# Groups four to seven of the first layer: from eight block products to seven in the first pass

## The chip, the cores and the metric

One core of one Trainium2 chip runs the whole program. The metric is the device time in microseconds (us) of one execution; the times below are of the same program executed several times.

## The reference

Attention without softmax, normed, and then two feed-forward blocks, all in float32:

```python
kv  = einsum('bhsd,bhse->bhde', k, v); out = einsum('bhsd,bhde->bhse', q, kv)   # 8 x 8 heads, 576 tokens, 64 wide
x   = out / sqrt(mean(out*out) + 1e-6) * g_norm                                 # then 4608 tokens x 512
h   = x @ w_in;  x = softplus(h) @ w_out                                        # 512 -> 2048 -> 512
h   = maximum(maximum(x @ w1, x @ w2), x @ w3);  y = h @ w2_out                 # 3 times 512 -> 768, then -> 512
```

## The kernel before, in words

The 4608 tokens are worked on in five passes of two half passes of 456 or 464 tokens (NS, L19). Every float32 operand is split in two parts, "hi" (a rounded copy) and "lo" (what is left), and a product is three matmuls: hi by hi, hi by lo, lo by hi (`mm3`, L150).

A layer is worked on in **groups** of 256 x 256 weights by the two half passes; a group is a 2 x 2 matrix of 128-row weight blocks a11, a12, a21, a22 times a 2 x 2 matrix of inputs. The first layer has eight groups H0 to H7 (numbers g = 0 to 7), the second eight, X00 to X31 (g = 8 to 15), the three of the second block nine (g = 16 to 24), the last layer three (g = 25 to 27). There are two ways to compute a group:

- **Plain**: eight block products. `plain_group` (L758) and `plain_sum` (L413) make each of the four results in a PSUM bank of its own, X and Y in turn, out of 12 matmuls (2 x 2 x 3). A group is 48 matmuls. Weights are a11, a12 (PLAIN[0]) and a21, a22 (PLAIN[1]), split as they are.
- **Seven products**: `run_group` (L403) and `product` (L390) run seven products of 6 matmuls in the order of ORDER (L37): m1 to bank X, m5 to bank Y, m6 on top of X, m2 to bank W, m7 on top of X, m4 on top of X, m3 on top of Y. A group is 42 matmuls. It takes sums of the weight blocks (`weight_sum`, L312, on GpSimd), sums of the inputs (`combine`, L370), and sums of results (`sums`, L424): after m1, m6 and m7 ScalarE copies bank X to SBUF before the next product goes on top of it, and VectorE adds banks W and Y later. SLOT (L36) places the products at 0, 1, 3, 4, 6, 9 and 12 steps from the group's start, and groups start 7 steps apart, so the last two products of a group stand between the first of the next.

In the first pass all groups are plain, and that pass also prepares the weights for the others: `convert` (L301) turns a raw double-precision block into float32 (two ScalarE and two VectorE instructions), `split_blocks` (L337) splits the plain blocks, `sums_of_weights` (L324) makes the four sums of a group in place, further `split_blocks` split the sums, and `keep_blocks` (L343) stores every split block to DRAM. Passes two to five load these units (`load_unit`, L206) and run all groups with seven products.

The order of the work is written out by hand. Everything is an event with a time in steps (`at`, L177); the events are issued in order of time. Up to t = 1 a string of names (OPENING, L43) sets the order on all engines, groups H0 to H2 of the first pass among them; after it the SP queue (all loads and stores) goes in order of events, and the other engines in the order that the scheduler gives at build time, earlier events first among those that it holds for ready. `order` (L737) places the groups of the first pass; `weights_at` (L708) places the weights' work around a group's start t; `x_plain`, `h_plain` (L774) evict results: ScalarE's softplus in the bank, ScalarE's cast to hi, VectorE's subtraction to lo. `plain_out` (L946) is the last layer of the first pass. Rings of buffers: PSUM banks X 2, Y 2, W 1, at 2, cv 1 (L100); two-block weight tiles "u" 4; weight sums "sw" 3; raw blocks 3; the inputs' tiles "xc" 28, the layer results' "gc" 28, the short-lived "c" 10.

In a row's names X, Y and W are the banks, followed by h for the first layer, x for the second, o for the three of the second block and y for the last.

Of the kernel before, what the change touches and what calls it, by code (L numbers as in the profile page):

```python
# [8 lines left out]
F32 = mybir.dt.float32  # L9
# [28 lines left out]
U_BUFS, U3_BUFS, GE_BUFS = 4, 2, 14  # L38
LATE = 23
OPEN, PIN, GATE = -100, 1, 24  # L40
ENGINES = tuple(getattr(mybir.EngineType, e) for e in ("PE", "Activation", "DVE", "Pool", "SP"))
LEAD = 10
OPENING = """  # L43
# [21 lines left out]
def kernel(  # L65
# [36 lines left out]
    def psum(tag, name):  # L102
        return ps.tile([P, 512], F32, tag=tag, bufs=PS_BUFS[tag], name=name)
# [4 lines left out]
    def ctile(name, n, dtype=F32):  # L108
        return wide(cp, "c", 10, name, n, dtype)
# [4 lines left out]
    def gc_tile(name, n, dtype=F32):  # L114
        return wide(gp, "gc", 28, name, n, dtype)
# [18 lines left out]
    def cast(eng, hi, src):  # L134
        if eng is nc.scalar:
            nc.scalar.copy(hi, src)  # L136
        else:
            eng.tensor_copy(hi, src)

    def split(eng_hi, src, hi, lo, eng_lo):  # L140
        cast(eng_hi, hi, src)
        eng_lo.tensor_tensor(out=lo, in0=src, in1=hi.bitcast(F32), op=ALU.subtract)  # L142
# [4 lines left out]
    def sub(eng, o, a, b):  # L147
        eng.tensor_tensor(out=o, in0=a, in1=b, op=ALU.subtract)  # L148
# [16 lines left out]
    def with_table(name, out, src, func, **kw):  # L165

        if tables["set"] != name:
            with after(tables["used"]):
                load = nc.scalar.preload_act_table_set(name)
            tables.update(set=name, load=load.ins, used=[])  # L170
        with after([tables["load"]]):
            tables["used"].append(nc.scalar.activation(out, src, func, **kw).ins)
# [4 lines left out]
    def at(t, fn, *args):  # L177
        events.append((t, len(events), fn, args))
# [14 lines left out]
    def unit_tile(size, p, own=False):  # L193
        if own and "ge" in pools:
            uxs.append(pools["ux"] if "ux" in pools and len(uxs) % 2 else pools["ge"])
            return uxs[-1].tile([P, 2, 512], F32R, tag="ux", bufs=1, name="ux")
        if size == 2:
            return up.tile([P, 2, 512], F32R, tag="u", bufs=U_BUFS, name="u")
        return up.tile([P, 1, 512], F32R, tag="u3", bufs=U3_BUFS, name="u3")

    def keep(key, u):
        n = u.shape[1] * 512
        wd[key] = dr.tile([P, n], F32, tag=f"wd{len(wd)}", name=f"wd{len(wd)}")
        nc.sync.dma_start(out=wd[key], in_=u.rearrange("p i n -> p (i n)").bitcast(F32))
# [36 lines left out]
    def raw_of(g):  # L241
        if g < 8:
            return [w_in[2 * g + i] for i in range(2)]
        if g < 16:
            return [w_out[2 * (g - 8) + i] for i in range(2)]
        if g in G_O:
            return [w2_out[2 * (g - G_O[0]) + i] for i in range(2)]
        f, j = divmod(g - 16, 3)
        return [w123[2 * f + i, j] for i in range(2)]
# [9 lines left out]
    def rebase(key, halves=(0, 1), tag=None):  # L259

        raw = raws[key]
        lo32, hi32 = raw[:, :, 0], raw[:, :, 1]
        if 0 in halves:
            t = parts[key] = psum(tag or ("W" if key[1] and key[0] < 17 else "cv"), "cv")
            nc.scalar.activation(t, hi32.bitcast(F32), AF.Copy, scale=2.0**-112)
        if 1 in halves:
            nc.scalar.activation(lo32, lo32.bitcast(U32), AF.Copy, scale=LOW_SCALE, bias=LOW_BIAS)
# [18 lines left out]
    sw = {}  # L286
# [50 lines left out]
    def split_blocks(g, ms, eng):  # L337

        u = unit_tile(len(ms), 0)
        split(nc.scalar, blocks_of(g, ms), u[:, :, 0:256], u[:, :, 256:512], eng)  # L340
        plain[g, ms] = u

    def keep_blocks(g, ms, of):  # L343
        u = plain[g, of]
# [58 lines left out]
    def run_group(base, p, g, rhs, after, slot=SLOT):  # L403
        banks = {}

        def step(m):
            product(p, g, m, rhs, banks)
            after(m, {k: v[:, 0:NS[p]] for k, v in banks.items()})

        for m in sorted(ORDER, key=slot.get):  # L410
            at(base + slot[m], step, m)
# [242 lines left out]
    def x_tiles(pas, c):  # L654
        a, n = TOK[pas], NS[pas]
        return [og_t[a + t * n, c + 2 * r] for r in range(2) for t in range(2)]
# [45 lines left out]
    def run_pass(pas, base):  # L702
# [3 lines left out]
        R = xc.setdefault(pas, {})  # L706

        def weights_at(t, g, slot=SLOT):  # L708
            if pas == 0:
                if g not in (0, 1, 2, 8):  # L710
                    for i in range(2):
                        jobs.append((t - 6 + 2.7 * i, (g, i), raw_of(g)[i], convert, (g, i)))
                    at(t - 3.4, split_blocks, g, PLAIN[0], nc.vector)
                    at(t - 0.6, split_blocks, g, PLAIN[1], nc.vector)
                if g > 1:
                    at(t + 0.2, sums_of_weights, g)
                if g >= LATE:
                    at(t + 4, keep_sums, g)
                    return
                if g < 2:  # L720
                    return
                for ms, dt in (((5, 6), 2.6), ((7,), 3.8), ((3,), 4.6)):
                    at(t + dt, split_blocks, g, ms, nc.gpsimd)
                    at(t + dt + 2.9, keep_blocks, g, ms, ms)
                if g not in (2, 8):
                    at(t + 0.5, keep_blocks, g, (1, 2), PLAIN[0])
                    at(t + 3, keep_blocks, g, (4,), PLAIN[1])
            else:
                for k, ms in enumerate(UNITS):

                    own = k == 0 and g != 17
                    lead = (8 if g == 0 else 5.9 if pas == 1 else 9) if own else LEAD
                    at(t + min(slot[m] for m in ms) - lead, load_unit, pas, (g, k), len(ms), own)
# [1 line left out]
        order = ["H0", "H1", "H2", "H3", "X00", "X01", "H4", "H5", "X10", "X11", "H6", "H7",  # L735
                 "X20", "X21", "X30", "X31"]
        if pas == 0:  # L737
            order = ["H0", "H1", "H2", "X00", "X01", "H3", "H4", "X10", "X11", "H5", "H6", "X20", "H7", "X21",
                     "X30", "X31"]
        start = {name: base + 7 * i for i, name in enumerate(order)}  # L740

# [16 lines left out]
        def plain_group(t, g, rhs, done, halves_first=False):  # L758
            outs = [(i, k) for i in range(2) for k in range(2)]
            if halves_first:  # L760
                outs = [(i, k) for k in range(2) for i in range(2)]

            def step(i, k, tag):
                done(i, k, plain_sum(g, i, k, rhs, tag))

            for n, (i, k) in enumerate(outs):
                at(t + 1.75 * n, step, i, k, "XY"[n % 2])

        def split_here(acc, tile):
            hi, lo = tile("hi", N, F32R), tile("lo", N, F32R)  # L770
            split(nc.scalar, acc, hi, lo, nc.vector)
            return hi, lo

        def h_plain(fp, i, k, acc):  # L774
            with_table(PLUS_SET, acc, acc, AF.Softplus)
            gc.setdefault(fp // 2, {})[i, k, fp % 2] = split_here(acc, xc_tile if fp == 7 else gc_tile)

        for fp in range(8):
            t = start[f"H{fp}"]
            weights_at(t, G_H[fp])  # L780
            if pas == 0:
                if fp > 2:
                    plain_group(t, G_H[fp], R0, partial(h_plain, fp))
                continue
            run_group(t, pas, G_H[fp], R, sums(lambda w, src, fp=fp: h_done(fp, w, src), lambda w: (ctile(f"h{w}", N), w != 11),
                           nc.vector if fp == 0 else nc.scalar))
# [158 lines left out]

        def plain_out(t):  # L946
            for j, (g, ts, split_at, sums_at) in enumerate(zip(
                    G_O, ((-8.6, -7), (-5, -3.2), (2, 4.5)), ((-6.2, -4.8), (-1.9, 0.1), (5.3, 7.05)), (1, 3.5, 9))):
                for i in range(2):
                    jobs.append((t + ts[i], (g, i), raw_of(g)[i], convert, (g, i)))  # L950
                    at(t + split_at[i], split_blocks, g, PLAIN[i], nc.vector if (j, i) == (1, 1) else nc.gpsimd)
                at(t + sums_at, sums_of_weights, g)
                at(t + sums_at + 3, keep_out, g)
            for n in range(8):
                e, i, k = n // 4, n // 2 % 2 if n > 3 else n % 2, n % 2 if n > 3 else n // 2 % 2
                at(t + 2.63 * n, out_plain, e, i, k, "XY"[n % 2])
                at(t + 2.63 * n + 5, out_store, e, 11 + 10 * i + k)
# [58 lines left out]

    def x_lo(k, eng):
        h, p = divmod(k, NP)
        low(eng, *tile_of.pop(k), og_t.pop((h * n0, p)))

    def low(eng, hi, lo, src):
        sub(eng, lo, src, hi.bitcast(F32))
# [177 lines left out]
```

## Time and profile before

| what | value |
|---|---|
| device time, median of 3 | 1377.56 us (1376.12 to 1379.06) |
| the profiled execution: its own time | 1378.63 us |
| its span, first to last instruction | 1376.8 us |
| TensorE busy in the span | 1359.8 us (99%), 6646 matmuls |
| VectorE, ScalarE, GpSimd busy | 826.7, 753.4, 649.6 us |
| data moved by DMA | 336.59 MB, mean 244 GB/s |

The span is what the profile sees; 1.8 us of the execution lie outside it. PE is TensorE's matmuls, DVE VectorE, ACT ScalarE, POOL GpSimd, SP the queue that issues the DMAs. A busy TensorE is not proof of TensorE at its best, since its matmuls overlap; the step from one matmul's start to the next is the better measure.

### The profile page before, as it was taken

To read this page: it belongs to the slowest core of one execution; us is meant where nothing else is said; L and a number is where in the kernel's file an instruction comes from. 1 tells how busy PE (TensorE), PEld (TensorE's weight loads), DVE (VectorE), ACT (ScalarE), POOL (GpSimd) and SP (SyncE) were. 2 spreads that over 40 slices of the span, in tenths; PEclk is the share of its full clock that TensorE was granted. 3 is DMA by queue.
4 is the path that set the end of the run, shared out by engine and by line. 5 is a ranking of instruction groups with operands and counts; after the bars stand their busy time and mean duration, and the time that the engine had idled before them with its cause. 6 is when DMAs were issued, how large, how long until landed. Compare 5 with 4: busy or idle time off the path is not lost.

```text
span 1376.8 us, 19727 instructions
## 1 busy us (share of the span) xinstructions
PE 1359.8 (99%) x6646; PEld 1212.5 (88%) x6646; DVE 826.7 (60%) x1307; ACT 753.4 (55%) x1461; POOL 649.6 (47%) x611
## 2 busy tenths in 40 slices
PE   8999999999999999999999999999999999999998
PEld 6799999888888888888888988888888889998897
DVE  6866657884445766745546667445567754457544
ACT  6786637884655457546444575464346645443332
POOL 3876545666555535335346253453334534445320
PEclk9999999999999999999999999999999999999999
DMA  8699868877899777586667764866676577666665
GB/s 302 226 340 310 313 237 296 273 248 253 300 333 329 263 271 247 169 301 211 214 213 251 259 210 161 295 212 214 208 225 198 188 259 236 212 206 204 219 199 171
DMA packets 132084, 336.59 MB, mean 244 GB/s; under 512 B 14224, under 2 KB 34576, under 8 KB 131984
## 3 DMA queue, kind: packets, MB, share of 16 engines
q1 hardware_dynamic: 131408, 334.36, 72.8%
q8 instruction: 53, 0.87, 0.3%
q10 hardware_dynamic: 576, 0.98, 0.2%
q14 instruction: 47, 0.39, 0.1%
HBM read 269.88 MB, written 65.40 MB: 244 GB/s over the span
## 4 chain that ended last, share of the span: by engine, by line
PE 88%; DMA 4%; DVE 3%; ACT 3%; POOL 1%; issue 1%; SPq 0%; DVEq 0%; ACTq 0%; POOLq 0%
PE Xx L152 5%; PE Xx L154 5%; PE Xx L153 5%; PE Xo L152 5%; PE Xh L152 5%; PE Xh L154 5%; PE Xh L153 5%; PE Xo L154 5%; PE Xo L153 5%; PE Yx L154 3%; PE Yx L153 3%; PE Yx L152 3%; PE Yh L152 3%; PE Yh L154 3%; PE Yh L153 3%; PE Yo L152 2%
## 5 line engine op out<-in xcount | busy, mean ns | idle before, releaser
L142 POOL TENSOR_TENSOR lo<-e,hi 128x464 fp32r<-128x464 f32 (+1 forms) x160 | 187.1, 1203 | 178.1 <-ACT hi L136 171.4
L136 ACT CAST hi<-t 128x464 fp32r<-128x464 f32 (+1 forms) x120 | 65.4, 546 | 114.9 <-DVE e L148 44.1
L152 PE MATMUL Xo<-hi,u 128*128 128x464 f32 (+1 forms) x296 | 111.6, 378 | 0.0
L154 PE MATMUL Xo<-hi,u 128*128 128x464 f32 (+1 forms) x296 | 110.0, 372 | 0.4 <-DVE u L142 0.4
L153 PE MATMUL Xo<-lo,u 128*128 128x464 f32 (+1 forms) x296 | 109.8, 371 | 0.0
L152 PE MATMUL Xh<-hi,u 128*128 128x464 f32 (+1 forms) x262 | 97.7, 373 | 2.9 <-DVE lo L148 1.7
L142 DVE TENSOR_TENSOR lo<-t,hi 128x464 fp32r<-128x464 f32 (+1 forms) x120 | 75.9, 637 | 38.3 <-ACT hi L136 36.0
L136 ACT COPY m<-Xo 128x464 f32<-128x464 f32 (+1 forms) x108 | 58.4, 546 | 73.0 <-PE Xo L154 72.8
L145 DVE TENSOR_TENSOR x<-x,Xx 128x464 f32<-128x464 f32 (+1 forms) x104 | 65.6, 632 | 52.9 <-PE Xx L154 52.6
L153 PE MATMUL Xh<-lo,u 128*128 128x464 f32 (+1 forms) x262 | 97.1, 371 | 0.0
L154 PE MATMUL Xh<-hi,u 128*128 128x464 f32 (+1 forms) x262 | 97.1, 370 | 0.0
L136 ACT CAST hi<-e 128x464 fp32r<-128x464 f32 (+1 forms) x160 | 85.4, 581 | 19.7 <-PE Yx L153 16.3
L152 PE MATMUL Xx<-hi,u 128*128 128x464 f32 (+1 forms) x256 | 95.1, 372 | 0.0
L154 PE MATMUL Xx<-hi,u 128*128 128x464 f32 (+1 forms) x256 | 94.9, 371 | 0.0
L153 PE MATMUL Xx<-lo,u 128*128 128x464 f32 (+1 forms) x256 | 94.8, 370 | 0.0
L142 POOL TENSOR_TENSOR u<-sw,u 128x256 fp32r<-128x256 f32 (+1 forms) x68 | 69.1, 1031 | 38.2 <-ACT u L136 38.1
L142 POOL TENSOR_TENSOR lo<-m,hi 128x464 fp32r<-128x464 f32 (+1 forms) x40 | 47.8, 1214 | 79.9 <-ACT hi L136 79.9
L148 POOL TENSOR_TENSOR e<-e 128x464 f32<-128x464 f32 (+1 forms) x32 | 38.0, 1189 | 99.4 <-DVE t L148 99.4
L136 ACT CAST u<-sw 128x512 fp32r<-128x512 f32 (+1 forms) x119 | 62.3, 537 | 37.2 <-POOL sw L148 16.3
L148 POOL TENSOR_TENSOR sw<-sw 128x256 f32<-128x256 f32 x84 | 67.9, 810 | 29.6 <-DVE sw L277 25.2
L650 POOL TENSOR_TENSOR og<-og,r 128x464 f32<-128x464 f32 (+1 forms) x32 | 40.4, 1262 | 70.6 <-DVE r L646 69.3
L145 DVE TENSOR_TENSOR Wh<-h,Wh 128x464 f32<-128x464 f32 (+1 forms) x32 | 20.6, 644 | 88.0 <-PE Wh L154 69.6
(261 smaller groups left out, 4165.7 us busy)
## 6 DMA issues: line engine op xcount, KB each, us to landing
u<-wd SPq DMA_DIRECT2D x241, 512.0 KB, 4.5
ux<-wd SPq DMA_DIRECT2D x99, 512.0 KB, 3.6
wd<-u SPq DMA_DIRECT2D x161, 256.0 KB, 4.6
u<-wd SPq DMA_DIRECT2D x104, 256.0 KB, 4.1
raw<-in_w_out_dram SPq DMA_DIRECT2D x22, 512.0 KB, 5.4
k<-in_kp_dram SPq DMA_DIRECT2D x31, 320.0 KB, 4.2
v<-in_vp_dram SPq DMA_DIRECT2D x29, 320.0 KB, 5.0
raw<-in_w_dram SPq DMA_DIRECT2D x18, 512.0 KB, 4.8
```

Of the source, the lines that this page charges most:

```text
L136: nc.scalar.copy(hi, src)
L142: eng_lo.tensor_tensor(out=lo, in0=src, in1=hi.bitcast(F32), op=ALU.subtract)
L145: eng.tensor_tensor(out=o, in0=a, in1=b, op=ALU.add)
L148: eng.tensor_tensor(out=o, in0=a, in1=b, op=ALU.subtract)
L152: nc.tensor.matmul(acc, wh, xh, start=first, stop=False, skip_group_check=on)
L153: nc.tensor.matmul(acc, wh, xl, start=False, stop=False, skip_group_check=on)
L154: nc.tensor.matmul(acc, wl, xh, start=False, stop=last, skip_group_check=on)
L650: nc.gpsimd.tensor_tensor(out=og, in0=og, in1=r, op=ALU.mult)
```

## The change

In the first pass groups 3 to 6 of the first layer (H3 to H6) are computed with seven products. For that `x_sums` makes the sums of the first pass's inputs, once for each c of 0 and 1; the groups' weight sums move ahead of the group and the seven blocks are split as units of two (`make_unit`), which are both used and stored, in place of the plain blocks and the sums apart; the results take the path of `sums` with `h_seven`. The last of X2's groups comes ahead of H7. Conversion uses other PSUM tags. Around the last layer, the sums of group 24 and of the last layer's groups, and their stores, move to later steps, conversion and split of the last layer's third group too, and the second group's first split moves from GpSimd to VectorE. Cut to what is spoken of:

```diff
+SEVEN = (3, 4, 5, 6)
...
-            t = parts[key] = psum(tag or ("W" if key[1] and key[0] < 17 else "cv"), "cv")
+            t = parts[key] = psum(tag or ("at" if key[1] and key[0] < 16 else "cv"), "cv")
...
+    def make_unit(g, k):
+        ms = UNITS[k]
+        u = unit_tile(len(ms), 0)
+        j = PLACE[ms[0]]
+        eng = nc.gpsimd if k else nc.vector
+        cast(nc.scalar if k < 2 else nc.gpsimd, u[:, :, 0:256], sw[g][:, j:j + len(ms)])
+        sub(eng, u[:, :, 256:512], sw[g][:, j:j + len(ms)], u[:, :, 0:256].bitcast(F32))
+        units[0, (g, k)] = u
+
+    def keep_first(key):
+        keep(key, units[0, key])
...
         def weights_at(t, g, slot=SLOT):
-            if pas == 0:
+            if pas == 0 and g in SEVEN:
+                for i in range(2):
+                    jobs.append((t - 9 + 3 * i, (g, i), raw_of(g)[i], convert, (g, i)))
+                at(t - 4.2, sums_of_weights, g)
+                for k, dt in enumerate((-2.6, -1, 1, 3)):
+                    at(t + dt, make_unit, g, k)
+                    at(t + dt + 2.4, keep_first, (g, k))
+            elif pas == 0:
...
                 if g > 1:
-                    at(t + 0.2, sums_of_weights, g)
+                    at(t + (0.2 if g < 24 else 5.5), sums_of_weights, g)
                 if g >= LATE:
-                    at(t + 4, keep_sums, g)
+                    at(t + (4 if g < 24 else 9), keep_sums, g)
...
-            order = [..., "H6", "X20", "H7", "X21",
+            order = [..., "H6", "X20", "X21", "H7",
...
-            gc.setdefault(fp // 2, {})[i, k, fp % 2] = split_here(acc, xc_tile if fp == 7 else gc_tile)
+            gc.setdefault(fp // 2, {})[i, k, fp % 2] = split_here(acc, gc_tile)
+
+        def h_seven(fp, w, src):
+            with_table(PLUS_SET, src, src, AF.Softplus)
+            hi, lo = gc_tile("hi", N, F32R), gc_tile("lo", N, F32R)
+            split(nc.scalar, src, hi, lo, nc.gpsimd if w == 22 else nc.vector)
+            gc.setdefault(fp // 2, {})[w // 10 - 1, w % 10 - 1, fp % 2] = (hi, lo)
...
+            if pas == 0 and fp in SEVEN:
+                run_group(t, pas, G_H[fp], R, sums(partial(h_seven, fp), lambda w: (gc_tile(f"h{w}", N), w == 22)))
+                continue
             if pas == 0:
                 if fp > 2:
-                    plain_group(t, G_H[fp], R0, partial(h_plain, fp))
+                    plain_group(t, G_H[fp], R0, partial(h_plain, fp), fp == 7)
...
-                    G_O, ((-8.6, -7), (-5, -3.2), (2, 4.5)), ((-6.2, -4.8), (-1.9, 0.1), (5.3, 7.05)), (1, 3.5, 9))):
+                    G_O, ((-8.6, -7), (-5, -3.2), (3, 5)), ((-6.2, -4.8), (-1.9, 0.1), (7.3, 8.8)), (2, 5, 10))):
...
-                    at(t + split_at[i], split_blocks, g, PLAIN[i], nc.vector if (j, i) == (1, 1) else nc.gpsimd)
+                    at(t + split_at[i], split_blocks, g, PLAIN[i], nc.vector if j == 1 else nc.gpsimd)
                 at(t + sums_at, sums_of_weights, g)
-                at(t + sums_at + 3, keep_out, g)
+                at(t + sums_at + 6, keep_out, g)
...
+    def x_sums(c):
+        b11, b12, b21, b22 = x_tiles(0, c)
+        dst = xc.setdefault(0, {})
+        for m, (i, k) in {1: (0, 0), 2: (1, 0), 3: (1, 1)}.items():
+            dst[m, c] = R0[i, k, c]
+        t1, t2 = (psum("at", "t")[:, 0:n0] for _ in range(2))
+        sub(nc.vector, t1, b12, b11)
+        sub(nc.vector, t2, b22, t1)
+        for m, t in ((5, t1), (6, t2)):
+            dst[m, c] = ctile("hi", n0, F32R), ctile("lo", n0, F32R)
+            split(nc.scalar, t, *dst[m, c], nc.vector)
+        sub(nc.gpsimd, b12, b22, b12)
+        sub(nc.vector, b11, b21, t2)
+        for m, t in ((7, b12), (4, b11)):
+            dst[m, c] = xc_tile("hi", n0, F32R), xc_tile("lo", n0, F32R)
+            split(nc.scalar, t, *dst[m, c], nc.gpsimd)
+
+    for c in range(2):
+        at(22 + 5 * c, x_sums, c)
```

## Rows read from the trace of the kernel before

**Rows 1.** Page, part 1: busy us, share of the span, instructions.

```profile
PE 1359.8 (99%) x6646; PEld 1212.5 (88%) x6646; DVE 826.7 (60%) x1307; ACT 753.4 (55%) x1461; POOL 649.6 (47%) x611
```

**Rows 2.** Waits of PE: who <- for whom: us in total, times, longest us.

```profile
PE Xh L152 <- DMA ux<-wd: 1.9, 1, 1.9
PE Xh L152 <- DVE lo L148: 1.7, 1, 1.7
...
PE Xy L154 <- POOL u L142: 1.2, 1, 1.2
```

**Rows 3.** Stretches: us, then busy by engine (instructions), granted clock, DMA share, GB/s.

```profile
core 0: us, PE busy (x) PEld busy (x) DVE busy (x) ACT busy (x) POOL busy (x), PEclk, DMA share, GB/s
60.00:80.00 20.00, 18.29 (x89) 16.25 (x88) 12.90 (x19) 13.49 (x31) 18.53 (x25) 1.00 0.76 262
80.00:100.00 20.00, 20.00 (x99) 18.11 (x97) 14.87 (x21) 18.33 (x39) 15.30 (x18) 1.00 1.00 355
...
120.00:140.00 20.00, 20.00 (x99) 18.11 (x98) 12.55 (x20) 14.04 (x28) 11.64 (x14) 1.00 0.86 289
```

**Rows 4.** Timeline of PE, first matmuls of groups H3 and H4: start us, us.

```profile
85.69 0.37 PE L152 MATMUL Xh<-hi,u 128*128 128x456 f32 x1
...
95.64 0.37 PE L152 MATMUL Xh<-hi,u 128*128 128x456 f32 x1
```

**Rows 5.** Timeline of PE, second pass: first matmuls of m1 and m6 of H0.

```profile
335.89 0.37 PE L152 MATMUL Xh<-hi,u 128*128 128x464 f32 x1
...
338.41 0.37 PE L152 MATMUL Xh<-hi,u 128*128 128x464 f32 x1
```

**Rows 6.** Page, part 5: busy us, mean ns | idle before, releaser.

```profile
L136 ACT COPY m<-Xo 128x464 f32<-128x464 f32 (+1 forms) x108 | 58.4, 546 | 73.0 <-PE Xo L154 72.8
...
L142 POOL TENSOR_TENSOR lo<-m,hi 128x464 fp32r<-128x464 f32 (+1 forms) x40 | 47.8, 1214 | 79.9 <-ACT hi L136 79.9
...
L145 DVE TENSOR_TENSOR Wh<-h,Wh 128x464 f32<-128x464 f32 (+1 forms) x32 | 20.6, 644 | 88.0 <-PE Wh L154 69.6
```

**Rows 7.** Groups of POOL, each shape by itself, 60 to 105 us: busy us, mean ns.

```profile
L148 POOL TENSOR_TENSOR sw<-sw 128x256 f32<-128x256 f32 x17 | 12.8, 758 | 5.0 <-DVE sw L277 4.1
...
L142 POOL TENSOR_TENSOR u<-sw,u 128x512 fp32r<-128x512 f32 x5 | 6.5, 1299 | 1.0 <-ACT u L136 1.0
```

**Rows 8.** Timeline of POOL, 58 to 86 us, where it had been idle [us <- releaser].

```profile
59.11 1.99 POOL L148 TENSOR_TENSOR u<-sw,u 128x512 fp32r<-128x512 f32 x2 [3.18 <-DMA raw<-in_w_out_dram]
61.58 0.61 POOL L138 CAST u<-sw 128x512 fp32r<-128x512 f32 x1 [0.47 <-PE Yh L154]
...
80.82 0.74 POOL L148 TENSOR_TENSOR sw<-sw 128x256 f32<-128x256 f32 x1 [1.35 <-DVE sw L277]
...
85.35 0.74 POOL L145 TENSOR_TENSOR sw<-sw 128x256 f32<-128x256 f32 x1 [0.69 <-DVE u L142]
```

**Rows 9.** Splitting a weight unit: timeline of ACT and DVE; all such splits, min/median/max ns.

```profile
81.46 0.62 ACT L136 CAST u<-sw 128x512 fp32r<-128x512 f32 x1
...
82.21 1.15 DVE L142 TENSOR_TENSOR u<-sw,u 128x512 fp32r<-128x512 f32 x1
...
L142 DVE TENSOR_TENSOR u<-sw,u x43: 679/693/1730, 72.1 to 311.1; 128x512 fp32r<-128x512 f32 x43
```

**Rows 10.** Waits of ACT, 60 to 200 us: us in total, times, longest us.

```profile
ACT u L136 <- POOL sw L148: 14.0, 11, 3.0
ACT u L136 <- DMA wd<-u: 9.2, 6, 2.1
...
ACT cv L265 <- DMA raw<-in_w_in_dram: 3.6, 3, 2.3
```

**Rows 11.** Timeline of POOL and PE at the first result of the last layer.

```profile
298.43 1.84 POOL L148 TENSOR_TENSOR sw<-sw 128x256 f32<-128x256 f32 x2
...
307.60 1.26 POOL L142 TENSOR_TENSOR u<-sw,u 128x512 fp32r<-128x512 f32 x1
...
308.91 0.48 PE L154 MATMUL Xy<-hi,u 128*128 128x456 f32 x1 [1.17 <-POOL u L142]
```

More of the change, by code (lines that the diff above doesn't have):

```diff
@@ L737, in run_pass @@
         if pas == 0:
-            order = ["H0", "H1", "H2", "X00", "X01", "H3", "H4", "X10", "X11", "H5", "H6", "X20", "H7", "X21",
+            order = ["H0", "H1", "H2", "X00", "X01", "H3", "H4", "X10", "X11", "H5", "H6", "X20", "X21", "H7",
                      "X30", "X31"]
@@ L1018, in x_lo @@
         h, p = divmod(k, NP)
-        low(eng, *tile_of.pop(k), og_t.pop((h * n0, p)))
+        low(eng, *tile_of.pop(k), og_t[h * n0, p])
+    def x_sums(c):
[16 more added lines that the diff above has]
+        at(22 + 5 * c, x_sums, c)
     def low(eng, hi, lo, src):
```

## The prediction

> **What bounds the kernel now.** I read the page's first part to find the bound, then PE's waits to see what is left beside it, then the stretches around the groups that change, and last the queues of ACT, DVE and POOL there. PE is busy for 1359.8 of 1376.8 us [rows 1]. PE's waits on other engines add up to little, and only three of them are above a microsecond between the end of the opening and the second pass [rows 2]: 1.7 us at the last result of H2, 1.2 us in the last layer of the first pass, 1.9 us for a load at the start of the second. So the time is the number of matmuls times their step, and a matmul removed is worth its step as long as nothing comes late. The step is read from the starts of two neighbouring groups, not from the 0.37 us that a row gives for one matmul, because matmuls overlap: H3 starts at 85.69 and H4 at 95.64, 48 matmuls later [rows 4], so 9.95 / 48 = 0.2073 us. The granted clock is 1.00 of full speed in all these stretches [rows 3], the 2.4 GHz level, and PE has no pause there that could lower it.
>
> **Part 1, the matmuls.** A plain group has 48, a group in seven products 42. Four groups: 24 x 0.2073 = 4.98 us less. The Trainium skill (TensorE: Matmul & The Clock Gate, section Back-to-back issue gap) gives a warm gap of columns / 2.4 GHz + 2.5 ns for a matmul by itself, 192.5 ns for 456 columns, and by it the part would be 4.62 us and the end 0.36 us later; the same page says that in a stream with weight loads the spacing goes by both. The row is 15 ns above the simple rule, and I go by the row.
>
> **Part 2, the results.** Every group in seven products adds three copies of bank X on ACT (0.546 us each) and three additions on DVE (0.644 us each) [rows 6]; softplus, cast and subtraction stay four each. Against that ACT casts two units in place of five pieces and DVE splits one unit in place of two. In the middle of the pass DVE and ACT are busy for 12.55 and 14.04 of 20 us, around H3 for 14.87 and 18.33 [rows 3], so it lies beside PE. What is new is how soon the copy is wanted: m6 goes on top of the bank of m1 and m7 on that of m6, with only one other product of 1.26 us between (half of the step from m1 to m6 [rows 5]), while a plain result has its bank for itself until two results later. Where a group in seven products follows another, products of the first stand between as well; but H3 and H5 begin alone. In the second pass's H0, which also begins alone, m6 follows without a gap [rows 5], there with a copy on DVE. I take 0, with a bound above in the second rival, and none below, since a copy can't make a matmul shorter.
>
> **Part 3, the sums of x.** Per c: three operations on POOL, one of them a subtraction and two lo parts, at 1.214 us [rows 6]; for both c 6 x 1.214 = 7.3 us of POOL. DVE gets ten and ACT eight of about 0.6 us, beside idle time of 7.1 and 6.5 us in 60 to 80 us [rows 3]: a tight fit, but X00 and X01 use plain banks, and their weights are split a group ahead. POOL has no such room: it is busy 18.53 of 20 us there.
>
> **Part 4, the weights of H3.** Plain H3 needs no weight sum; now its first unit (m1, m5) needs the first two. The chain from the converted block, POOL 2 x 0.758 [rows 7], cast 0.62, subtraction 1.15 [rows 9], is 3.3 us. The first sum of this group is at 80.82 now, as soon as its block is there (the releaser is the conversion) [rows 8]; 80.82 + 3.3 = 84.1, 1.6 us ahead of PE's 85.69. But the sums of x stand ahead of it in POOL's order. They have 1.35 us of idle time just before 80.82, and those of c = 1, which nothing ties to the end of the opening, may have 3.18 + 0.47 us at 59 to 61 us [rows 8]. If they use none of the latter, the start is 7.3 - 1.35 = 5.95 us late and PE waits 5.95 - 1.6 = 4.35 us. If they use all, PE waits 5.95 - 3.65 - 1.6 = 0.7 us. A split of the previous group's sums that is only stored (1.3 us [rows 7]) may get ahead as well: 5.65 us at most; at the other end 0, if the order puts H3's sums first. I take the middle of 0.7 and 4.35, **2.5 us**, because idle time in the opening is only usable where the order was made to see it. Later units and H4 follow a POOL that needs about 8 us per group (four sums, two subtractions at 1.3, two casts, a small subtraction, a lo part) against 42 x 0.2073 = 8.7 us of PE: no further wait. The sums need no longer wait for the plain split, which held POOL for 0.69 us [rows 8]; that goes into POOL's idle time. H5 and H6 meet a POOL busy 11.64 of 20 us [rows 3]: 0.
>
> DVE's subtraction takes 0.69 us at the median, but 1.15 in this place and up to 1.73 us, where POOL works beside it [rows 9]. The Trainium skill (SBUF — State Buffer, section SBUF: two separate sides) has DVE operations with two SBUF inputs and GpSimd operations exclude each other for whole instructions; the rows bear that out. By it this subtraction could wait out one POOL operation, 0.69 + 0.76 = 1.45 us, which makes the wait 2.8 and the sum 1374.2; by the row it is as summed.
>
> **Part 5, the last layer.** PE waits 1.17 us before 308.91 for a split that POOL does from 307.60 for 1.26 us, behind the sums of group 24 and of group 25 [rows 11]. Both sums move later and this split moves to DVE, which is busy 60% over the span [rows 1]. So 1.17 us goes; next late is the third group's split, due four results on. Bounds 0 and 1.17. The stores of the last sums now come behind the first load of the second pass on SP, which can only help that load; the loads behind them are tied to PE's last matmuls, so the 1.9 us wait [rows 2] stays.
>
> **Part 6, edits with one answer.** X21 ahead of H7, the PSUM tags, the "gc" tiles for H7, four stores of the same bytes in place of six: PE's cover is its own queue, with no wait in any of these places [rows 2]; if it goes, the first to show is X30 waiting for H7's last results.
>
> **The sum.** -4.98 - 1.17 + 2.5 = -3.65 us. On the profiled execution that is 1378.63 - 3.65 = 1375.0 (span 1373.2); that execution is 1.07 us above the median, so for the median 1377.56 - 3.65 = **1373.9 us**. The lateness alone between 1.1 and 4 us gives this case a range of 1372.5 to 1375.4.
>
> **Rivals.** (A) *POOL in time.* The order lets H3's sums go first. Then -6.15 us: 1371.4. For it: the stored-only splits of groups 2, 8 and 9 can wait. Against it: they hold weight buffers, and POOL is 93% busy. (B) *POOL becomes the bound.* All sums of x and a stored-only split are ahead: wait 5.65 us, -0.5 us: 1377.1. For it: 18.53 of 20 us [rows 3], and events with earlier times go first. Against: the 3.65 us of idle time. (C) *ACT's queue holds bank X.* ACT goes in order and already waits there for POOL's sums and for stores that free a weight buffer, 14.0 + 9.2 us in 17 waits, 1.36 us each, and for raw blocks up to 2.3 us [rows 10]; now no PE wait follows because results have spare banks. If the copy after m1 and m6 stands behind such a wait and one more operation, PE waits 1.36 + 0.55 + 0.55 - 1.26 = 1.2 us; two places in each of four groups: 9.6 us, so 9.6 - 6.15 = 3.45 us slower: 1381.0. It decides from a backlog of 1.26 - 0.55 = 0.7 us on. For it: ACT at 18.33 of 20 us around H3. Against: at H5 only 70%, and in two of each four groups more products stand between.
>
> **Chances.** A measurement of this kernel can tell 0.2% from no change, 2.75 us, so faster means below 1374.8 and slower above 1380.3. Forecast 0.47, A 0.17, B 0.20, C 0.16. Faster: A and four fifths of the forecast's case, 0.56. Same: the rest of that and nearly all of B, 0.26. Slower: C and a little of B with further waits at H4, 0.18. The range goes from A's time with 0.4 us for the small DVE waits before the last layer, 1371.0, to above B, 1379.5, and leaves out C.
>
> **What would show it.** Right: 24 matmuls fewer; the four groups 34.8 in place of 39.8 us apart from waits; one wait at H3's first matmul of 1 to 4 us with DVE's u or POOL's sums as releaser; no wait of PE at Xy; the ux wait unchanged. A is shown by no wait at H3, B by POOL without idle time from 62 us to H4, C by waits of PE at m6 and m7 with ACT's copy as releaser. The forecast is wrong if the waits in H3 to H6 add up to over 6 us, or if a wait appears where none is now: X01's weights, the bank after H4 or H6, or X30.

## The result, and the profile after

| | device time, median (us) | ratio to the kernel before |
|---|---|---|
| before, beside it | 1377.82 (1376.12 to 1381.28, 6 runs) | |
| changed | 1388.50 (1385.44 to 1390.53, 6 runs) | 1.0079 [1.0067, 1.0091] |

Slower by 10.7 us where 3.65 us less was forecast. The changed kernel's profiled execution has a span of 1387.8 us, 11.0 more than before. Part 1 of its page, to be read against [rows 1]:

```profile
PE 1362.2 (98%) x6622; PEld 1210.1 (87%) x6622; DVE 834.7 (60%) x1322; ACT 760.9 (55%) x1469; POOL 665.9 (48%) x628
```

The 24 matmuls are gone, and their step is what it was: from 114.63 to 184.28 us PE issues 336 matmuls, 0.2073 us each, as in [rows 4]. So the saving of 4.98 us was made, and some 16 us came on top. To find them I cut the span at the first matmul of each stage (worked out from PE's timeline; us):

| | to X00 | X00 to second block | second block | last layer | pass 2 | the rest |
|---|---|---|---|---|---|---|
| before | 65.8 | 132.6 | 106.2 | 31.2 | 264.2 | 776.7 |
| changed | 65.4 | 142.2 | 107.6 | 29.9 | 266.2 | 776.5 |

Nearly all lies in the second column: from X00 to X10 the changed kernel takes 49.25 us for 168 matmuls (H4's last 12 stand behind X10's first), 14.4 more than 168 steps, where before 192 took 39.77, which is 192 steps. PE's waits in the changed kernel from 56 to 350 us (who <- for whom: us in total, times, longest):

```profile
PE Xh L155 <- POOL u L149: 3.4, 1, 3.4
PE Xh L153 <- DMA u<-wd: 2.1, 1, 2.1
PE Xh L153 <- ACT u L137: 2.0, 2, 1.1
PE Xx L153 <- ACT u L137: 1.7, 1, 1.7
PE Xh L155 <- DVE u L149: 1.3, 1, 1.3
PE Xx L155 <- DVE u L143: 1.1, 2, 0.9
...
```

Of the six lines shown, all but the second lie between 75 and 106 us, in X01, H3 and at the start of H4, and add up to 9.6 us there. They are waits for weights (the tile "u"), where [rows 2] has none in this stretch. The second is at the start of pass 2. Xy's wait for POOL is gone, as predicted.

Waits are not all. The stretches that answer to [rows 3], and two of two microseconds each (columns as there):

```profile
60.00:80.00 20.00, 16.86 (x77) 14.28 (x77) 13.26 (x19) 12.88 (x30) 17.77 (x22) 0.97 0.56 187
80.00:100.00 20.00, 14.18 (x59) 11.49 (x58) 12.91 (x19) 12.46 (x25) 18.14 (x22) 0.93 0.84 286
100.00:120.00 20.00, 18.85 (x85) 16.66 (x84) 11.59 (x20) 14.79 (x29) 12.95 (x16) 0.93 0.75 258
...
80.00:82.00 2.00, 2.00 (x7) 1.75 (x6) 1.93 (x4) 0.78 (x2) 1.70 (x2) 0.50 0.00 0
...
100.00:102.00 2.00, 2.00 (x6) 1.75 (x6) 0.00 (x0) 0.44 (x2) 1.76 (x3) 0.50 0.88 360
```

The granted clock (the column after POOL's) was 1.00 here before. Now it is 0.97, 0.93 and 0.93, and in the two microseconds behind the waits in X01 and in H3 it is 0.50, the 1.2 GHz level. 20 us times 0.03, 0.07 and 0.07 is 3.4 us, most of what is left of the 14.4 beside 9.6 us of waits. Note also that from 80 to 100 us ACT and DVE are less busy than before (12.46 and 12.91 us against 18.33 and 14.87 in [rows 3]), though they have more to do: they stand waiting too.

For whom? ACT, DVE and POOL around 70 us, one view each of the changed kernel's timeline (start us, us, engine and line, operation, in brackets the idle time before and its releaser):

```profile
68.61 0.51 ACT L820 COPY x<-Xx 128x456 f32<-128x456 f32 x1
73.41 0.58 ACT L137 CAST hi<-og 128x456 fp32r<-128x456 f32 x1 [4.28 <-POOL og L149]
73.89 0.54 ACT L137 CAST hi<-t 128x456 fp32r<-128x456 f32 x1
...
75.98 1.15 ACT L137 CAST u<-sw 128x512 fp32r<-128x512 f32 x2
```

```profile
74.46 0.63 DVE L143 TENSOR_TENSOR lo<-t,hi 128x456 fp32r<-128x456 f32 x1 [4.27 <-ACT hi L137]
```

```profile
69.55 2.69 POOL L143 TENSOR_TENSOR u<-sw,u 128x512 fp32r<-128x512 f32 x3
72.20 1.18 POOL L149 TENSOR_TENSOR og<-og 128x456 f32<-128x456 f32 x1
```

b22 - b12 of `x_sums` (og<-og) is on POOL, behind three splits of weights. ACT, which goes in order, has the cast of its result next and stands for 4.28 us; behind that cast wait the other casts of x, the copies of X00's results and, at 75.98, two casts of weights, one of them X01's, for which PE waits. In the kernel before, DVE had these weights of X01 done at 73.02 us, 2.7 us ahead of X01's first matmul at 75.76:

```profile
72.10 0.92 DVE L142 TENSOR_TENSOR u<-sw,u 128x512 fp32r<-128x512 f32 x1 [1.84 <-ACT u L136]
```

POOL in H3, of the changed kernel:

```profile
90.05 0.74 POOL L146 TENSOR_TENSOR sw<-sw 128x256 f32<-128x256 f32 x1
...
93.93 0.73 POOL L143 TENSOR_TENSOR u<-sw,u 128x256 fp32r<-128x256 f32 x1
94.63 0.74 POOL L149 TENSOR_TENSOR sw<-sw 128x256 f32<-128x256 f32 x1
95.32 0.74 POOL L143 TENSOR_TENSOR u<-sw,u 128x256 fp32r<-128x256 f32 x1
96.02 0.73 POOL L146 TENSOR_TENSOR sw<-sw 128x256 f32<-128x256 f32 x1
96.83 1.53 POOL L149 TENSOR_TENSOR sw<-sw 128x256 f32<-128x256 f32 x2
98.32 1.26 POOL L149 TENSOR_TENSOR u<-sw,u 128x512 fp32r<-128x512 f32 x1
```

The second sum, which H3's first unit needs, is made at 90.05 us, where the prediction's chain had it at 81.6, right behind the first sum of [rows 8]: 8.5 us late. Most of that isn't POOL's queue. The sums need H3's second block, the twelfth that is converted, and DVE finishes it 6.5 us later than before: its conversion stands in ACT's queue too, and starts there at 84.11 us where it did at 78.07. The kernel before, then the changed one:

```profile
80.06 0.69 DVE L277 SCALAR_TENSOR_TENSOR sw<-raw,cv 128x512 int32<-128x512 int32 x1
```

```profile
86.56 0.69 DVE L278 SCALAR_TENSOR_TENSOR sw<-raw,cv 128x512 int32<-128x512 int32 x1
```

The other 2 us are POOL's, for sums of X01's group. The subtraction at 98.32 is H3's second unit, and PE waits 3.44 us for it. Ahead of it, from 93.93 us on, POOL makes the four sums of H4, wanted half a group later, and two splits that are only stored. In the order of events the unit stands first (`make_unit` at t - 1, H4's sums at t + 7 - 4.2); the order on POOL is the scheduler's.

### The profile page after: what moved, and what is told of

The parts are those of the page before. It is cut to its first block, busy times and chain, and to the rows that moved or that the text cites. A ratio compares the mean times of both kernels' runs of the same rounds, so it can differ in the third digit from the quotient of the medians.

```text
span 1387.8 us, 19685 instructions
## 1 busy us (share of the span) xinstructions
PE 1362.2 (98%) x6622; PEld 1210.1 (87%) x6622; DVE 834.7 (60%) x1322; ACT 760.9 (55%) x1469; POOL 665.9 (48%) x628
## 4 chain that ended last, share of the span: by engine, by line
PE 87%; DVE 4%; ACT 3%; DMA 3%; POOL 2%; issue 1%; SPq 0%; POOLq 0%; DVEq 0%; ACTq 0%
PE Xo L153 5%; PE Xo L155 5%; PE Xo L154 5%; PE Xh L153 5%; PE Xh L155 5%; PE Xh L154 5%; PE Xx L153 4%; PE Xx L154 4%; PE Xx L155 4%; PE Yx L153 3%; PE Yx L155 3%; PE Yx L154 3%; PE Yo L153 3%; PE Yo L155 3%; PE Yo L154 3%; PE Yh L153 2%
## 5 line engine op out<-in xcount | busy, mean ns | idle before, releaser
L143 POOL TENSOR_TENSOR u<-sw,u 128x256 fp32r<-128x256 f32 (+1 forms) x55 | 55.3, 1015 | 40.1 <-ACT u L137 40.1
L173 ACT ACTIVATE e<-h 128x464 f32<-128x464 f32 (+1 forms) x64 | 37.9, 592 | 60.5 <-DVE h L146 59.6
```

## The experiments

Ratios are to the kernel before on the same chip, with 95% intervals. The kernel before took 1376.93 to 1377.82 us on the different chips, so runs are best compared by their ratios.

**The rest without the groups, and the late two.** Two runs from the changed kernel:

```diff
-SEVEN = (3, 4, 5, 6)
+SEVEN = ()
...
-    for c in range(2):
-        at(22 + 5 * c, x_sums, c)
```

> The changed kernel without any group in seven products and without the sums of x; the last-layer part and the new order stay. Theory 1 (the loss is made by the sums of x and the units of H3 and H4, in the stretch where POOL is full): all waits between 72 and 106 us are gone, the Xy wait of 1.2 us too, the load waits at the start of the second pass are 2 to 3 us in place of 1.9: 1377.8 - 1.2 + 0.5 = about 1377, within 1.5 us. Theory 2 (the form itself costs, and the last-layer part costs as well): above 1379.5.

Measured: 1382.16 us, 1.0035 [1.0023, 1.0048]. Without any group in seven products the change costs 4.8 us by itself. That is theory 2's time, but not its causes: the form isn't in this kernel, and the last-layer part costs next to nothing alone (below). In the profiled execution, 3.9 us longer than that of the kernel before, 2.0 us lie ahead of X00, where PE waits 2.2 us for H2's last result and the granted clock is 0.50 behind it (64 to 66 us), and 1.8 us between X00 and the second block, with waits of 0.5 and 0.7 us in X30. The single parts follow below. The second run:

```diff
-SEVEN = (3, 4, 5, 6)
+SEVEN = (5, 6)
-        at(22 + 5 * c, x_sums, c)
+        at(44 + 6 * c, x_sums, c)
```

> Only H5 and H6 in seven products, the sums of x at steps 44 and 50 in place of 22 and 27. Theory 1: 12 matmuls fewer are 2.5 us, no wait of PE above 0.5 us in H5 and H6 and none in X01 and H3: 2.5 us below the run without groups in seven products, about 1374.5. Theory 2 (the copies of bank X and the POOL work per group cost wherever they stand): waits at m6 and m7 of 1 us each, 1376 to 1379.

Measured: 1382.58 us, 1.0035 [1.0021, 1.0048]: the same, so 12 matmuls fewer (2.5 us) bought nothing. In H5, ACT and PE:

```profile
132.89 0.63 ACT L266 ACTIVATE cv<-raw 128x512 f32<-128x512 f32 x1 [1.56 <-DMA raw<-in_w_out_dram]
133.45 0.65 ACT L268 ACTIVATE raw<-raw 128x512 int32<-128x512 uint32 x1
134.00 0.53 ACT L137 COPY h<-Xh 128x456 f32<-128x456 f32 x1
```

```profile
134.67 0.44 PE L153 MATMUL Xh<-hi,u 128*128 128x456 f32 x1 [1.57 <-ACT h L137]
```

The copy of bank X stands behind a conversion that waits for its load: the mechanism of the prediction's rival C, at its place (a product on top of the bank) and near its size of 1.2 us. A second one of 0.88 us is at 141 us, in H6.

**One subtraction to VectorE, and the last layer put back.** Each from the changed kernel:

```diff
-        sub(nc.gpsimd, b12, b22, b12)
+        sub(nc.vector, b12, b22, b12)
```

> As the changed kernel, but the subtraction b22 - b12 of the sums of x runs on DVE in place of POOL. Theory 1a (ACT goes in order and stood 4.3 us behind this POOL operation, so that X01's weights came late): ACT's wait before the cast of og is under 1 us, X01's waits of 1.7 + 0.9 us and the low clock around 80 us are gone; H3's waits stay at 3 to 5 us: 1384 to 1386. Theory 1b (POOL's backlog alone decides): X01's waits stay within 0.7 us of 2.6: 1388.

Measured: 1382.25 us, 1.0038 [1.0027, 1.0049], some 6 us less than the change for one subtraction per c; in the profiled executions 5.3 us of it lie between X00 and the second block (136.9 against 142.2 us). ACT's stand before the cast is 0.92 us, X01's waits shrink to 0.28 us, and the clock's fall behind them is gone. This shows ACT's stand behind POOL to be the cause of the waits in X01. Waits remain in H3 and at the start of H4 (3.06 and 2.56, then 0.59 us). DVE has H3's second block done at 83.17 us here, 4 us earlier than in the changed kernel, and POOL's first sum of it starts 3.3 us after that, behind sums of X01's group, a stored-only split and a lo part of x: what is left of the first wait is the backlog of POOL that part 4 of the prediction summed.

The second run takes back all hunks of the change around the last layer, among them

```diff
-                    at(t + (0.2 if g < 24 else 5.5), sums_of_weights, g)
+                    at(t + 0.2, sums_of_weights, g)
-                at(t + sums_at + 6, keep_out, g)
+                at(t + sums_at + 3, keep_out, g)
```

> As the changed kernel, but the times around the last layer (sums of group 24, conversion, splits, sums and stores of the last three groups) are those of before. If the later stores hold the second pass's loads on SP: the 2.1 us wait for a load at the second pass's first group is gone or under 0.5, a Xy wait of about 1.2 us and the 1.9 us ux wait are back: within 0.7 us of the changed kernel, 1388. If the last-layer part is a gain of its own: 1389.5.

Measured: 1385.73 us, 1.0056 [1.0043, 1.0070], 3 us less than the change. Xy waits 1.2 us again; in its place the wait of 2.1 us for a load goes, which in the changed kernel reads so on SP's queue and on PE:

```profile
339.01 5.72 SPq L377 DMA_DIRECT2D wo<-sw  x5
344.83 0.45 SPq L209 DMA_DIRECT2D u<-wd  x1
```

```profile
349.90 0.45 PE L153 MATMUL Xh<-hi,u 128*128 128x464 f32 x1 [2.11 <-DMA u<-wd]
```

Five stores of the last sums hold SP's queue for 5.72 us, 2.2 of which SP waits for POOL to make the sums, and a load of pass 2 stands behind them.

**All four groups relieved.** Both edits, the splits of x for products 7 and 4 in an event of their own, and group 9's splits that are only stored 5 steps later:

```diff
-        for m, t in ((7, b12), (4, b11)):
-            dst[m, c] = xc_tile("hi", n0, F32R), xc_tile("lo", n0, F32R)
-            split(nc.scalar, t, *dst[m, c], nc.gpsimd)
+    def x_more(c, m):
+        b11, b12, b21, b22 = x_tiles(0, c)
+        d = xc[0][m, c] = xc_tile("hi", n0, F32R), xc_tile("lo", n0, F32R)
+        split(nc.scalar, b12 if m == 7 else b11, *d, nc.gpsimd)
...
+        at(34.2, x_more, c, 7)
+        at(36.2, x_more, c, 4)
```

> All four groups in seven products, last-layer times as before; b22 - b12 on DVE, the lo parts of the sums for m7 and m4 on POOL only at steps 34.2 and 36.2 (behind H3's first weight units), the stored-only splits of group 9 five steps later. Theory A (POOL's queue ahead of H3's weight sums makes H3's waits): the waits in H3 and H4, 6.2 us with b22 - b12 alone on DVE, fall under 2 us and the clock stays full: 1382.25 - 2.8 (last layer) - 4 = about 1375.5. Theory B (raw blocks and ACT are late there anyway): waits of 4 us or more remain, 1379 to 1381.

Measured: 1391.25 us, 1.0101 [1.0084, 1.0118], no better than the change, and 8 us worse than the run with the first two edits alone (below). PE's waits from 62 to 200 us are a dozen small ones, up to 2.5 us long, 4.0 us in sum for POOL's subtractions and 2.9 for its casts. H3's are 5.4 us of them, not under 2; the longest stands in H5, whose second unit POOL subtracts at 137.89 us, right behind the four sums of H6, as in H3 of the changed kernel. Theory A is out; which of the moved pieces made the new waits wasn't tried.

**The late two with DVE's copies.** From the changed kernel: SEVEN = (5, 6), x_sums at 44 + 6c, last layer and order of H7 and X21 as before, and

```diff
-run_group(t, pas, G_H[fp], R, sums(partial(h_seven, fp), ...))
+run_group(t, pas, G_H[fp], R, sums(partial(h_seven, fp), ..., nc.vector))
```

> Only H5 and H6 in seven products, sums of x at steps 44 and 50, last layer and order of H7 and X21 as before, and the copies of bank X on DVE in place of ACT. Theory A (in the run with two groups the copies stood behind ACT's waits for raw blocks, 1.6 + 0.9 us, and X30 behind H7): no wait of PE in H5, H6 and X30 above 0.4 us: 1377.6 - 2.5 = 1375.1. Theory B (DVE is as late as ACT): waits of 1 us or more at m6 or m7, 1376.5 to 1379.

Measured: 1382.74 us, 1.0042 [1.0027, 1.0058]. Bank X waits again (1.78 us at 131 us, under m6 of H5), now for DVE's copy, ahead of which DVE works without a pause from 127.97 us on conversions, additions and a split of weights: an engine that converts weights in order holds the bank, whichever of the two it is.

**The parts of the rest, each alone on the kernel before.** First the hunks around the last layer, in the sense of the change:

> The kernel before with only the times around the last layer changed. Theory A (the later stores hold the second pass's loads on SP): the Xy wait of 1.2 us is gone, a wait of 1 to 2.5 us for a load u at the second pass's first group is there, the sum is 1.5 to 3 us slower than before, 1379 to 1380.5. Theory B (they only cost beside the other parts): 1376.5.

Measured: 1378.26 us, 1.0005 [0.9996, 1.0014]. Xy's wait is gone, a load wait of 0.9 us is new: no gain. Then the order, with H7's tiles:

```diff
-            order = [..., "H6", "X20", "H7", "X21",
+            order = [..., "H6", "X20", "X21", "H7",
...
-split_here(acc, xc_tile if fp == 7 else gc_tile)
+split_here(acc, gc_tile)
...
-plain_group(t, G_H[fp], R0, partial(h_plain, fp))
+plain_group(t, G_H[fp], R0, partial(h_plain, fp), fp == 7)
```

> The kernel before with only X21 ahead of H7 and H7's tiles in the results' ring. Theory A (X30 then waits for H7's last results, 0.5 + 0.7 us in the run without groups in seven products): 1 to 1.7 us slower than before, 1378.6 to 1379.3. Theory B (that wait came with something else): no wait at X30, 1377.6 within 0.7.

Measured: 1381.73 us, 1.0028 [1.0018, 1.0039], 3.9 us slower. Waits of PE, 150 to 200 us:

```profile
PE Yx L152 <- ACT hi L136: 1.9, 1, 1.9
PE Yx L153 <- DVE lo L142: 0.7, 1, 0.7
PE Xx L152 <- DVE lo L142: 0.6, 1, 0.6
```

X30 waits for H7's last results, which now come right before it, and the granted clock of 180 to 200 us is 0.91. The profiled execution is the slowest of twelve (1385.19 us), so these rows show the place, and more than the usual size. Last, the banks:

```diff
-t = parts[key] = psum(tag or ("W" if key[1] and key[0] < 17 else "cv"), "cv")
+t = parts[key] = psum(tag or ("at" if key[1] and key[0] < 16 else "cv"), "cv")
```

> The kernel before with nothing but the other PSUM banks for conversion. The rest of the change cost 4.5 us without the seven products; the order of H7 and X21 alone cost 4.0, the last layer alone 0.7. Theory A, these add up and the banks cost nothing: 1377.2 to 1378.3 us. Rival B, at and cv are shared with the opening's work and delay H2's last result, which PE waits for at 61 us (2.2 us there with the banks changed, 1.7 before): 0.5 to 2.5 us slower, 1378.2 to 1380.2, with a wait of over 2 us at 61 us and a granted clock below 0.95 behind it.

Measured: 1376.78 us, 1.0004 [0.9995, 1.0013]. Theory A. The three parts add up to 0.37%, the whole without the groups cost 0.35%: by the times, the rest's cost is the order of X21 and H7. By place that is shown only in part. Without the groups X30's waits are 1.2 us, and the 2.0 us ahead of X00 are in none of the three parts alone (PE waits 0.97 to 1.80 us for H2's last result there, at a clock of 1.00).

**The two that helped, together; then H3 plain as well.** The second run, from the first:

```diff
-SEVEN = (3, 4, 5, 6)
+SEVEN = (4, 5, 6)
-        at(22 + 5 * c, x_sums, c)
+        at(29 + 5 * c, x_sums, c)
```

> The changed kernel with two of its parts put back at once: b22 - b12 of the sums of x on VectorE, the last layer's times as before. Theory A, the costs add up: each alone took 6.2 and 2.8 us off, so 1388.5 - 9.0 = 1379.5 us; no wait of PE in X01, waits of 4 to 6.5 us in H3, Xy's wait of 1.2 us back, the wait of 2 us for a load at the start of the second pass gone. Rival B, they share a cause (the stores pushed on by the late opening): then no more than the larger of the two, 1382.3.

Measured: 1383.19 us, 1.0043 [1.0031, 1.0055]: 5 us less than the change, so the two gains overlap, as rival B had it; that they share the cause it names wasn't tried.

> As the run before (b22 - b12 on VectorE, last layer as before), but H3 plain and the sums of x 7 steps later, so that only H4, H5 and H6 are in seven products (18 matmuls fewer, 3.7 us). Theory A, H3 stands too close to the sums of x and to its own weights' sums: without it the waits at 85 to 99 us (6.2 us and some 2 us of low clock) go, 1.25 us of matmuls come back, 1379.5 - 8.2 + 1.25 = 1372.6 us, and the kernel beats the one before. Rival B, the chain block, sums, units is too long for its lead wherever it comes first: H4 waits as H3 did, 3 us or more in its first and second products, 1378 to 1381. Rival C, bank X's copies behind ScalarE's waits and X30 waiting for H7 take it back, as with the two late groups: no wait at H4, but 1378 to 1382.

Measured: 1378.10 us, 1.0010 [1.0001, 1.0018]. H3 in this place cost 4.5 us net (0.33% of the time), less than theory A's 6.9, and the kernel before isn't beaten. From X00 to the second block the profiled execution takes 3.0 us more than before: 18 matmuls give 3.7 us, but H4's first product waits 2.1 us for the bank of H3's first result, m6 of H4 1.2 us for ACT's copy, and the granted clock of 0.94 and 0.89 around them is another 3.4 us (C, in H4). This kernel still has X21 ahead of H7, as all runs with H3 or H4 in seven products do; with the old order it wasn't run.

The third run, from the second:

```diff
-        at(before[-3] + 0.01, load_raw, key, src)
+        at(max(before[-3] + 0.01, t - 6 if key[0] == 10 else 0), load_raw, key, src)
```

> The run with three late groups, and the loads of group 10's raw blocks held back to 6 steps before their conversion, so that on ScalarE the conversion of a later group no longer stands ahead of H3's first softplus. There, PE waited 2.1 us at 93.4 us for bank X, and the granted clock was 0.94 and 0.89 in the 40 us around it. Theory A, ScalarE's order holds the banks: this wait goes and the clock is 1.00, so 1378.1 - 2.1 - 1.5 to 2 = 1374 to 1374.5 us, and it beats the kernel before by 0.2%. Rival B, the wait only moves to where the held-back work is wanted (H4's weights at about 98 us or X10's at 107): 1377 to 1380, with a new wait of 2 us or more there.

Measured: 1379.14 us, 1.0010 [1.0000, 1.0019]. Theory A is out, and the time is rival B's; but the wait hasn't moved. It is at H4's first product as before, 3.06 in place of 2.14 us. ACT, PE and POOL:

```profile
90.65 0.53 ACT L173 ACTIVATE Xh<-Xh 128x456 f32<-128x456 f32 x1
94.72 0.62 ACT L137 CAST u<-sw 128x512 fp32r<-128x512 f32 x1 [3.54 <-POOL sw L146]
95.24 0.53 ACT L137 CAST hi<-Xh 128x456 fp32r<-128x456 f32 x1
```

```profile
96.66 0.75 PE L153 MATMUL Xh<-hi,u 128*128 128x456 f32 x1 [3.06 <-DVE lo L143]
```

```profile
93.15 0.73 POOL L149 TENSOR_TENSOR sw<-sw 128x256 f32<-128x256 f32 x1
93.96 0.72 POOL L146 TENSOR_TENSOR sw<-sw 128x256 f32<-128x256 f32 x1
```

H3's softplus is early now, but between it and its own cast stands a cast of H4's weights, which waits 3.54 us for POOL's second sum. DVE's lo part follows ACT's cast, and PE follows DVE. The profile names DVE as releaser; the one late was POOL.

**The same kernel again, for the clock.** Two more executions of the kernel with two parts put back, unedited.

> The same kernel as the run with b22 - b12 on VectorE and the last layer as before, for a second look. Its profiled execution took 1379.95 us with a granted clock of 1.00 behind waits of 3.1 and 3.6 us in H3; its five others took 1383.0 to 1384.8. Theory A, the 3 us between are a stretch at the low clock behind the same waits, that one execution has and another not: an execution of 1383 us shows the same waits and granted clocks below 0.95 somewhere in 80 to 120 us, one of 1380 us shows 1.00. Rival B, the waits themselves differ: an execution of 1383 us shows 3 us more of waits and a clock of 1.00.

> A third look at the same kernel, with the same two theories: the time of the execution goes with the granted clock behind H3's waits (A), or with the sum of PE's waits (B).

Measured: 1384.78 and 1382.15 us. The stretch of 80 to 100 us of the earlier execution (1379.95 us) and of the one of 1384.78 us:

```profile
80.00:100.00 20.00, 12.61 (x57) 9.85 (x56) 9.67 (x16) 11.58 (x24) 17.23 (x21) 1.00 0.97 328
```

```profile
80.00:100.00 20.00, 14.42 (x54) 11.80 (x53) 8.31 (x13) 10.76 (x22) 17.64 (x21) 0.83 0.97 325
```

The first wait in H3 is 3.1 us in all three. Behind it the clock is 1.00 in one and 0.83 in two (the third reads as the second), and the second wait is 3.6, 2.4 and 2.3 us: PE comes later to a unit that POOL finishes when it does. From X00 to the second block it makes 136.7 against 138.2 and 139.3 us (the third has 0.75 us of wait in X01). So theory A holds for 1.5 to 2 us of the difference; the rest of the execution of 1384.78 us (1.2 us in the second block, 1.5 in pass 2, both at clock 1.00) is neither theory's and stays open. The times on record bear A out: of this kernel's first six executions the one of 1379.95 us has a mean granted clock of 1.000, the five of 1383.0 to 1384.8 us have 0.997 or 0.998. Over all executions it was 0.996 to 0.999 in the changed kernel and 0.998 to 1.000 in the one before.

## Why the prediction was wrong

**Matmuls (part 1): right**, in number and step; 0.2073 us, not the 0.1925 of the rule cited there from the Trainium skill (TensorE: Matmul & The Clock Gate, section Back-to-back issue gap), is what 336 matmuls without a wait took again.

**Sums of x (part 3): right in size, wrong in reach.** POOL's six operations take 7.5 us (two of 1.17, four of 1.29 in the mean) where 7.3 was summed. The step that failed is "X00 and X01 use plain banks, and their weights are split a group ahead". It misread the kernel: `weights_at` splits X01's blocks 3.4 and 0.6 of the group's 7 steps ahead, and the first were done only 2.7 us before X01. And I asked which engine has room, not who stands behind whom. ACT had 6.5 us of idle time in [rows 3] and lost 4.3 us of it at once behind b22 - b12, with X01's cast in its queue. Worth 6 us of the time by experiment.

**Weights of H3 (part 4): right in kind, mis-sized.** The forecast was one wait of 2.5 us, bounds 0 to 5.65. Measured were 0.89, 1.26 and 3.44 us in H3 and 1.15 at H4, 6.7 us. Two steps failed. The chain started "as soon as its block is there", with the block at its old time; it came 6.5 us later, and 4 us of that go with b22 - b12 on VectorE, where the first wait is 3.06 us, near the 2.5 forecast. And "Later units and H4 follow a POOL that needs about 8 us per group ... no further wait": a sum of work per group says nothing of its order, and H4's four sums stood ahead of H3's second unit.

**The clock: no term at all.** I had read that the granted clock was 1.00 because PE had no pause there, and did not ask what a forecast pause would do to it. Some 3.4 us in the changed kernel.

**Results (part 2): set at 0, right in the changed kernel, wrong in its variants.** Rival C's mechanism is shown at H5 and H6 (1.57 and 0.88 us), at H4 (1.2 us), and with DVE's copies (1.78 us). In the changed kernel itself H3 to H6 have no such wait: in H3 and at H4 the weights are later than the copies, in H5 and H6 nothing is late, and why the copies are in time there wasn't tried. So C was a true cost that comes out when other waits are taken away.

**Last layer (part 5): half right.** Xy's 1.17 us went. "The loads behind them are tied to PE's last matmuls" failed: with the groups in seven products the stores hold such a load, PE waits 2.11 us for it, and the ux wait is 0.80 in place of 1.87. Alone on the kernel before, the part is worth nothing.

**Order of X21 and H7 (part 6): set at 0.** Alone it costs 3.9 us, at the place the prediction named (X30 waits for H7). The changed kernel's profile has no wait there, so this part is not among its losses; why its ACT and DVE are in time there wasn't tried.

The sum by these steps, on the span: -4.98 for the matmuls, +9.6 waits and +4.8 clock and short steps behind waits from X00 to X10, +2.0 in pass 2, +1.4 in the second block (four short waits for three engines and a load, 1.1 us together, between 239 and 249 us; why they are late wasn't sought), -1.3 in the last layer, -0.4 before X00, -0.2 in the other passes: 10.9, against 11.0 measured. The range missed because every bound in it was that of one wait, at H3; several waits at once stood only in rival C, which was left out of the range, and the clock behind waits was in no case. Two of the signs that the text gave for being wrong came true: waits over 6 us in H3 to H6, and X01's weights.

Open: PE waits 2.0 to 2.3 us for H2's last result in three runs (no groups, and the two late ones with either engine's copies) and 0 to 1.8 us in all others. In those three alone the granted clock falls to 0.50 behind it, and X00 starts some 2 us later, which is about half of what the profiled execution of each of the three lost. In the first of them the order of the instructions up to there is that of the kernel before, so it may lie in the executions. A smaller slip of the prediction, on which nothing hangs: the chance of faster adds up to 0.55, not 0.56.

## What to carry to other kernels

Before moving work to an engine with idle time, write down for each of its results what stands behind the reader in the reader's own in-order queue: one subtraction of 1.2 us on POOL for each c cost 6 us because ACT stood behind it with another group's weights, and with the conversion of the next. When the bound is an engine that never pauses, price a wait with the clock that it may lose, and take a chain of short leads as several waits, not as the longest one. And try a plan's side edits alone: here one of them (the order of X21 and H7) cost 3.9 us by itself, where four groups in seven products save 4.98.

## What was not expected of the hardware

The granted clock falls behind waits in a busy stretch in some executions and not in others: behind the same wait of 3.1 us in the same kernel it was 1.00 once and 0.83 over 20 us twice.

DVE and POOL, in the changed kernel; each engine's timeline:

```profile
78.62 1.59 DVE L149 TENSOR_TENSOR t<-og 128x456 f32<-128x456 f32 x1
...
81.57 0.64 DVE L149 TENSOR_TENSOR t<-og,t 128x456 f32<-128x456 f32 x1
```

```profile
78.11 1.61 POOL L143 TENSOR_TENSOR lo<-og,hi 128x456 fp32r<-128x456 f32 x1
80.30 1.17 POOL L149 TENSOR_TENSOR og<-og 128x456 f32<-128x456 f32 x1 [0.58 <-DVE t L149]
```

The subtraction with both inputs in SBUF takes 1.59 us here, beside a POOL operation that takes 1.61 us; the same one for the other c took 0.82 us (at 67.37 us), and POOL's other lo parts of x 1.17 to 1.20 us. The subtraction with one input in PSUM takes 0.64 us, though POOL works then too (81.42 us, 1.43 us long). The Trainium skill (SBUF — State Buffer, section SBUF: two separate sides) says that the shared pair of ports is an exclusive lock and that the other engine "fully blocks"; these rows agree: both operations are lengthened, a sum of x as a split of weights is in [rows 9].
